# Pairs of batches in rows of their own: wider product matmuls, 64-row products with the states, four groups in place of five, and another tabulated order

## The chip, the cores and the metric

The kernel runs on one NeuronCore of a Trainium2 chip. The metric is the device time of one execution in microseconds (us). The engines are TensorE (PE for matmuls, PEld for the weight load ahead of each), VectorE (DVE), ScalarE (ACT), GpSimd (POOL) and SyncE (SP), whose queue issues nearly all DMAs.

## The reference, cut to what matters

Eight batches of eight heads; x is (8, 8, 512, 64), state (8, 8, 32, 64), all float32. An attention between tokens and states in both directions gives 544 rows of 512 per batch, and a soft mixture of experts runs over all 4352 rows.

```python
scores = x @ state.T / 8;  a  = softmax(scores);   xread = a @ state
scores2 = state @ x.T / 8; a2 = softmax(scores2);  sread = a2 @ x
x = concat([xread, sread], axis=2)             # then (B, S + Ns, H * D)
logits = x @ phi                               # 32 slots
d = softmax(logits over all rows)              # dispatch
slot_input = d.T @ x
slot_out[e] = relu(slot_input[e] @ w1[e]) @ w2[e]     # 8 experts, 4 slots each
out = softmax(logits over slots) @ slot_out    # combine
```

## The kernel before, in words

The kernel never forms xread. It folds the states into phi (`G`: state times phi, for every head), so that the logits of the tokens are G times the attention weights. The dispatch product d.T @ xread is taken in two steps as well: first the 32x32 blocks t = d.T @ a of each head (`T`), then t @ state (`Px`). The softmax over all rows is a running one: for each group of batches a new maximum, a factor that rescales what was summed so far, and an addition to the 128x128 tile `y`, which becomes the slot inputs.

Each batch b goes through steps, which are small functions. `X.b.g` transposes two heads of x on PE (g from 0 to 3) and `xe` copies them out on ACT; `S.b` makes the scores; then, for each half h of the heads, the token softmax (`q` transpose on DVE, `m1` maximum on DVE, `sub` on POOL, `x1` exponential on ACT, `l1`, `r1` on DVE, `mul` on POOL, `aT` transpose on DVE), the state softmax (`m2` on DVE, `e2` on ACT, `l2` on DVE) with its transposes (`E` on PE, `ee` on ACT) and its product with x (`R` on PE, then `sr`, `srT`, `srTe`), and the logits `Lx.b.h` on PE from `aT` and G. `A.b.h` transposes `aT` back on PE and `ae` copies it out on ACT, into one of two `an` buffers.

A group k of batches (the table `GROUPS`) then goes through `keep`, `mx` (maximum), `mk`, `bm`, `nme` (maximum over the rows of the array), `dx` (exponential on ACT), `dT`, `dTe` (transpose and copy), `T`, `tt` (transpose on DVE), `Px`, and `Y` (the addition to y). The state rows of four batches each go through a like chain (`Ls` to `Ys`). `Wd`, `We`, `Yf`, `SI`, `SIe` close the softmax and place the slot inputs in `si_m`; then come the expert matmuls `w1_half` (tile h_ps), `w2_part` (so_ps) and `out` (o).

What sets the order is `ORDER`, a written list of some 480 steps: each engine executes its instructions in the order in which this list issues them. Loads of expert weights are issued by SP as the buffers of x come free: `R.b.1` issues two of them, `load_half` puts three half sets into buffers of the attention, and the rest follow in the expert stage.

Of the kernel before, what the change touches and what calls it, by code (L numbers as in the profile page):

```python
# [34 lines left out]
X.3.0 r1.1.0 mul.1.0 xe.3.0 x1.1.1 A.0.1 R.1.0 Lx.0.0 m2.2.0 R.1.1 l2.1 Lx.0.1 X.4.1 e2.2.1 m1.2.0 sub.2.0
aT.1.0 E.2.1 q.2.1 ae.0.1 l1.1.1 A.1.0 e2.2.0 l2.2 ee.2.1 r1.1.1 xe.4.1 S.3 X.4.0 sr.1 srTe.0 m1.2.1 X.4.3
ae.1.0 m2.3.0 mul.1.1 aT.1.1 E.2.0 x1.2.0 xe.4.0 srT.1 l1.2.0 xe.4.3 U.0 m2.3.1 X.4.2 q.3.0 ee.2.0 sub.2.1
e2.3.0 Lx.1.0 R.2.0 srTe.1 q.3.1 Lx.1.1 Ue.0 R.2.1 sr.2 xe.4.2 m1.3.0 sub.3.0 A.1.1 E.3.0 e2.3.1 keep.0 X.5.3
r1.2.0 mx.0 m1.3.1 S.4 sub.3.1 x1.2.1 l1.2.1 m2.4.0 mk.0 bm.0 nme.0 srT.2 xe.5.3 X.5.2 m2.4.1 ee.3.0 x1.3.0
# [5 lines left out]
sub.5.1 E.5.0 l1.4.0 r1.4.1 msx.0 lkp.0 pv.1 V.0 sr.4 r1.4.0 dsx.0 l1.5.0 mul.4.0 x1.5.1 al.0 S.6 aT.3.1 m2.6.0
ee.5.0 Px.0 ee.5.1 Ve.0 l1.5.1 m2.6.1 r1.5.1 mul.5.1 mul.4.1 Y.0 R.5.0 r1.5.0 Lx.3.1 mx.1 l2.5 e2.6.0 keep.1
R.5.1 A.3.1 X.7.0 e2.6.1 ae.3.1 q.6.1 mk.1 srT.4 srTe.4 aT.5.1 sr.5 xe.7.0 X.7.1 xe.7.1 X.7.2 xe.7.2 bm.1 X.7.3
E.6.1 nme.1 dx.1 q.6.0 xe.7.3 al.1 als.0 srT.5 D.0 E.6.0 dT.1 srTe.5 dTe.1 m1.6.0 sub.6.0 pv.2 mul.5.0 aT.4.0
ee.6.0 x1.6.0 l2.6 m1.6.1 sub.6.1 S.7 aT.4.1 Lu.0 m2.7.1 C.0 Ce.0 A.5.1 Lx.4.0 m2.7.0 aT.5.0 T.1 ee.6.1 Lx.4.1
tt.1 R.6.0 e2.7.1 x1.6.1 l1.6.0 Lx.5.0 Ps.0 l1.6.1 ae.5.1 Lus.0 Lx.5.1 mx.2 R.6.1 e2.7.0 A.4.0 keep.2 E.7.0  # L50
r1.6.1 mul.6.1 E.7.1 mk.2 Ys.0 bm.2 ae.4.0 ee.7.0 sr.6 r1.6.0 mul.6.0 q.7.0 srT.6 A.4.1 nme.2 aT.6.1 m1.7.0
ee.7.1 U.1 aT.6.0 dx.2 pv.3 q.7.1 A.5.0 dT.2 l2.7 srTe.6 dTe.2 Lu.1 R.7.0 Lx.6.0 ae.5.0 R.7.1 sub.7.0 x1.7.0
Lx.6.1 keep.3 Px.1 ae.4.1 m1.7.1 sr.7 srT.7 mx.3 mk.3 Y.1 Ue.1 load_half A.6.0 bm.3 A.6.1 srTe.7 Ls.1 sub.7.1
x1.7.1 l1.7.0 r1.7.0 mul.7.0 nme.3 al.3 l1.7.1 al.2 Lse.1 r1.7.1 aT.7.0 T.2 dx.3 dT.3 dTe.3 Lr.1 ae.6.1 lkp.1
# [14 lines left out]
def attention_soft_moe(ctx: ExitStack, tc: tile.TileContext, x, stT, phi, w1, w2, out_x, out_s):  # L69
# [84 lines left out]
    with ExitStack() as actx:  # L154
# [27 lines left out]
        def G(b):  # L182
            R[0]["gp"] = p = ps_t.tile([P, B, 2 * NS], F32, tag="tr", name="g_ps")
            for b in range(B):
                for g in range(4):
                    pe.matmul(
                        p[32 * g : 32 * g + 32, b, :],
                        stT_sb[:, b, 32 * g : 32 * g + 32],
                        phi_bd[:, g].rearrange("p h n -> p (h n)"),
                        start=True,  # L190
                        stop=True,
                    )
# [25 lines left out]
        def Sc(b):  # L218
# [3 lines left out]
            for g in range(4):  # L222
                for h in range(2):
                    pe.matmul(  # L224
                        r[f"sp{h}"][32 * g : 32 * g + 32, :],
                        stT_sb[64 * h : 64 * h + 64, b, 32 * g : 32 * g + 32],
# [231 lines left out]
        def T_(k):  # L458
            r = X2[k]
            r["tp"] = mtile([P, len(r["b"]), 2, NS], f"t_ps{k}")  # L460
            for i, b in enumerate(r["b"]):
                for j in range(NJ):
                    for g in range(4):
                        pe.matmul(  # L464
                            r["tp"][32 * g : 32 * g + 32, i, :, :],
                            r["dT"][:, i, 32 * j : 32 * j + 32],
                            R[b]["an"][:, j, g],
# [4 lines left out]
        def tt(k):  # L472
            r = X2[k]
            r["tt"] = sm.tile([P, len(r["b"]), 2, NS], F32, tag="tt", name=f"tt_{k}", bufs=1)
            dve.transpose(
                r["tt"].rearrange("p i h n -> p (i h n)"), r["tp"].rearrange("p i h n -> p (i h n)")
# [12 lines left out]
        def Px(k):  # L489
            r = X2[k]  # L490
            r["pxp"] = p = mtile([P, 2, D], f"px_ps{k}")
            n = len(r["b"])
            for h in range(2):
                for g in range(4):
                    rows = slice(32 * g, 32 * g + 32)
                    for i, b in enumerate(r["b"]):
                        pe.matmul(
                            p[rows, h, :],
                            r["tt"][rows, i, h, :],
                            Q[b // 4]["st"][rows, b % 4, D * h : D * h + D],  # L500
                            start=(i == 0),
                            stop=(i == n - 1),
# [325 lines left out]
```

## Time and profile before

| | us |
|---|---|
| median of 3 timed runs (150.08 to 151.0) | 150.22 |
| the profiled execution, whole | 151.79 |
| its span in the trace | 150.0 |
| attention and dispatch: start to the first h_ps matmul | 93.1 |
| first expert matmuls (h_ps) | 14.25 |
| from there to the end | 42.7 |

| engine | busy us | share of the span | instructions |
|---|---|---|---|
| PE | 124.9 | 83% | 2083 |
| PEld | 93.9 | 63% | 2083 |
| DVE | 88.4 | 59% | 223 |
| ACT | 88.0 | 59% | 210 |
| POOL | 41.9 | 28% | 61 |

The shares are means over two unlike halves: up to 93 us all engines work side by side, and behind it DVE and ACT wait for PE and PE works through the expert weights. The mean granted clock of TensorE is 0.95. DMA moves 51.76 MB in all, and stands nearly still from 86 to 95 us.

### The profile page before, as it was taken

What the parts mean: (1) busy time and instruction counts of PE and PEld (TensorE: products, weight loads), DVE (VectorE), ACT (ScalarE), POOL (GpSimd) and SP (SyncE); (2) the same over time, 40 slices, a digit from 0 to 9 for tenths busy, and PEclk for the clock granted to TensorE, in tenths of its full rate; (3) what the DMA queues carried; (4) which work ended last, traced back from release to release, by engine and by line L of the source; (5) the groups of instructions that cost most, each with busy time, mean ns of one, the idle gap of its engine ahead of it and who ended that gap; (6) DMA issues with size and microseconds to landing.
All of it is one profiled execution on the core that took longest, in us unless ns stands there. A gap on an engine that the chain in (4) does not pass through costs nothing.

```text
span 150.0 us, 5037 instructions
## 1 busy us (share of the span) xinstructions
PE 124.9 (83%) x2083; PEld 93.9 (63%) x2083; DVE 88.4 (59%) x223; ACT 88.0 (59%) x210; POOL 41.9 (28%) x61
## 2 busy tenths in 40 slices
PE   0598939999999998599996787999999999988700
PEld 0567735977677856549874564999786656656500
DVE  2019990999799999759986216198220143356700
ACT  3149963996999985969984821206430445366700
POOL 3004543262555563381847120630000000000000
PEclk9999995999999999969999969999999999999985
DMA  4899999999999999999999800289999938668995
GB/s 120 289 387 402 420 414 421 413 420 415 414 415 415 418 416 417 416 418 413 404 402 304 317 20 2 82 298 390 421 420 415 421 152 352 281 256 350 418 420 238
DMA packets 15286, 51.76 MB, mean 345 GB/s; under 512 B 1696, under 2 KB 1952, under 8 KB 15264
## 3 DMA queue, kind: packets, MB, share of 16 engines
q1 hardware_dynamic: 15120, 51.39, 86.6%
q8 instruction: 16, 0.26, 0.7%
q10 hardware_dynamic: 144, 0.07, 0.2%
q14 instruction: 6, 0.05, 0.1%
HBM read 42.53 MB, written 8.91 MB: 343 GB/s over the span
## 4 chain that ended last, share of the span: by engine, by line
PE 68%; DVE 12%; issue 6%; ACT 6%; DMA 3%; SPq 0%; DVEq 0%; ACTq 0%
PE so_ps L701 10%; PE h_ps L646 9%; PE xt_ps L210 8%; PE sc L224 6%; PE o L731 6%; PE eT_ps L292 4%; PE an_ps L292 4%; PE sr_ps L317 4%; PE t_ps L464 3%; DMA x<-x_in 3%; ACT out L733 2%; PE lt L349 2%; PE cT_ps L686 2%; DVE q L237 2%; DVE l1s L253 2%
## 5 line engine op out<-in xcount | busy, mean ns | idle before, releaser
L210 PE MATMUL xt_ps<-ident,x 128*128 128x128 f32 x128 | 20.5, 303 | 9.5 <-DMA x<-x_in 5.6
L210 PEld LDWEIGHTS xt_ps<-ident,x 128*128 128x128 f32 x128 | 15.7, 154 | 14.5 <-issue 9.1
L215 ACT ACTIVATE xt<-xt_ps 128x512 f32<-128x512 f32 x32 | 18.5, 612 | 7.0 <-PE xt_ps L210 6.5
L262 POOL TENSOR_TENSOR q<-q,r 128x512 f32<-128x512 f32 x16 | 16.7, 1048 | 18.0 <-DVE r L258 10.5
L246 POOL TENSOR_TENSOR q<-q,m 128x512 f32<-128x512 f32 x16 | 16.7, 1049 | 16.5 <-DVE m L242 9.3
L273 DVE TENSOR_REDUCE nm<-sc 128x1 f32<-128x512 f32 x16 | 10.5, 667 | 12.2 <-PE sc L224 12.2
L735 DVE COPY out<-o 128x512 f32<-128x512 f32 x16 | 10.8, 689 | 9.6 <-PE o L731 9.6
L733 ACT COPY out<-o 128x512 f32<-128x512 f32 x18 | 10.3, 586 | 8.4 <-PE o L731 8.3
L701 PE MATMUL so_ps<-w,h_m 128*32 128x256 f32 x256 | 15.3, 382 | 0.0
L646 PE MATMUL h_ps<-w,si_m 128*32 128x512 f32 x128 | 14.2, 592 | 0.4 <-DVE si_m L624 0.4
L731 PE MATMUL o<-so,cT 128*128 128x256 f32 x68 | 12.7, 313 | 1.8 <-ACT out L733 0.9
L646 PEld LDWEIGHTS h_ps<-w,si_m 128*32 128x32 f32 x128 | 12.9, 110 | 1.0 <-DVE si_m L624 0.5
L731 PEld LDWEIGHTS o<-so,cT 128*128 128x128 f32 x68 | 9.4, 188 | 6.5 <-ACT out L733 2.4
L278 ACT ACTIVATE e<-sc,nm 128x512 f32<-128x512 f32 x16 | 11.3, 704 | 1.5 <-DVE q L237 1.2
L267 DVE STREAM_TRANSPOSE aT<-q 128x512 f32<-128x512 f32 x16 | 11.1, 692 | 1.6 <-PE eT_ps L292 0.8
L237 DVE STREAM_TRANSPOSE q<-sc 128x512 f32<-128x512 f32 x16 | 11.0, 690 | 1.0 <-ACT e L278 0.9
L309 ACT COPY an<-an_ps 128x512 f32<-128x512 f32 x16 | 9.3, 590 | 3.1 <-PE an_ps L292 3.1
L224 PE MATMUL sc<-xt,stT_sb 64*32 64x512 f32 x128 | 11.0, 690 | 0.0
L317 PE MATMUL sr_ps<-x,eT 128*32 128x64 f32 x512 | 10.5, 221 | 0.5 <-ACT eT L300 0.5
L701 PEld LDWEIGHTS so_ps<-w,h_m 128*32 128x32 f32 x256 | 7.7, 109 | 5.1 <-issue 0.3
L292 PE MATMUL eT_ps<-ident,e 128*128 128x128 f32 x64 | 10.1, 291 | 0.9 <-ACT e L278 0.5
L242 DVE TENSOR_REDUCE m<-q 128x16 f32<-128x512 f32 x16 | 10.6, 668 | 0.1
(127 smaller groups left out, 206.7 us busy)
## 6 DMA issues: line engine op xcount, KB each, us to landing
w<-w_in SPq DMA_DIRECT2D x61, 512.0 KB, 9.9
out_x<-out SPq DMA_DIRECT2D x16, 512.0 KB, 3.5
x<-x_in SPq DMA_DIRECT2D x14, 512.0 KB, 9.1
w<-w_in SPq DMA_DIRECT2D x6, 256.0 KB, 7.5
...
```

Source lines behind the costliest of these rows:

```text
L210: pe.transpose(p[:, P * j : P * j + P], xb[2 * b + g // 2][:, g % 2, j, :], ident)
L215: act.mul(r[f"xt{g}"], r[f"xp{g}"], 0.125)
L224: pe.matmul(r[f"sp{h}"][32 * g : 32 * g + 32, :], stT_sb[64 * h : 64 * h + 64, b, 32 * g : 32 * g + 32], r[f"xt{g}"][64 * h : 64 * h + 64, :],
L237: dve.transpose(r[f"q{h}"], r[f"sp{h}"])
L246: pool.tensor_tensor(v, v, R[b][f"m1{h}"].broadcast_to([P, 16, NS]), op=ALU.subtract)
L262: pool.tensor_tensor(v, v, R[b][f"r1{h}"].broadcast_to([P, 16, NS]), op=ALU.mult)
L292: pe.transpose(p[:, j, :], r[f"{src}{h}"][:, P * j : P * j + P], ident)
L317: pe.matmul(r["srp"][32 * g : 32 * g + 32, h, :], r[f"eT{h}"][:, j, 32 * g : 32 * g + 32], xb[2 * b + g // 2][:, g % 2, j, D * h : D * h + D],
L646: pe.matmul(h_ps[hf][32 * kt : 32 * kt + 32, :], si_m[kt // 2][:, 256 * (kt % 2) + 32 * e : 256 * (kt % 2) + 32 * e + 32], w1t[4 * e + kt] ...
L701: pe.matmul(so[hf][c4 : c4 + 32, :], h_m[ft // 4][:, 256 * (ft % 4) + 32 * e : 256 * (ft % 4) + 32 * e + 32], w2t[hf, e, ft], start=(e == ...
L731: pe.matmul(o[:, i, :], cT[b // 2][:, 4 * (b % 2) + j + i, :], so4[hf], start=True, stop=True)
L733: act.copy(ot[:, j : j + 2, :], o)
```

## The change

The change concerns the dispatch products `T` and `Px` and what they need. The last two batches, groups of their own before, become one pair, so there are four groups of two. In `T` the two batches of a pair no longer lie side by side in the free dimension, with the four head pairs g in the four row blocks of the output; now a row block of 32 holds (half of g, batch), and the two g of a half lie side by side in the free dimension. A matmul therefore streams 128 columns instead of 64, and there are half as many. In `Px` the two batches lie under each other in 64 contraction rows, so the sum over the pair, which took two accumulating matmuls, takes one. For this the states are stored in another order (`stT_in`, read through `st_t`), and the first of their two loads holds two batches (128 KB) in place of one (64 KB). `Y`, `mx`, `dx` and the others are as before, four times instead of five.

```diff
-GROUPS = ((0, 1), (2, 3), (4, 5), (6,), (7,))
+GROUPS = ((0, 1), (2, 3), (4, 5), (6, 7))
...
-    stT_sb = big.tile([P, B, P], F32, tag="big", name="stT_sb")
+    stT_sb = big.tile([P, 4, 2, 2, 2, NS], F32, tag="big", name="stT_sb")
...
+    def st_t(b, g):
+        return stT_sb[:, b // 2, g % 2, g // 2, b % 2, :]
...
-            r["tp"] = mtile([P, len(r["b"]), 2, NS], f"t_ps{k}")
-            for i, b in enumerate(r["b"]):
-                for j in range(NJ):
-                    for g in range(4):
+            r["tp"] = mtile([P, 2, 2, NS], f"t_ps{k}")
+            for j in range(NJ):
+                for gh in range(2):
+                    for i, b in enumerate(r["b"]):
+                        row = 64 * gh + 32 * i
                         pe.matmul(
-                            r["tp"][32 * g : 32 * g + 32, i, :, :],
+                            r["tp"][row : row + 32, :, :, :],
                             r["dT"][:, i, 32 * j : 32 * j + 32],
-                            R[b]["an"][:, j, g],
+                            R[b]["an"][:, j, 2 * gh : 2 * gh + 2],
...
-            for h in range(2):
-                for g in range(4):
-                    rows = slice(32 * g, 32 * g + 32)
-                    for i, b in enumerate(r["b"]):
+            for g2 in range(2):
+                for h in range(2):
+                    for gh in range(2):
+                        g = 2 * gh + g2
+                        rows = slice(64 * gh, 64 * gh + 64)
                         pe.matmul(
-                            p[rows, h, :],
-                            r["tt"][rows, i, h, :],
-                            Q[b // 4]["st"][rows, b % 4, D * h : D * h + D],
-                            start=(i == 0),
-                            stop=(i == n - 1),
+                            p[32 * g : 32 * g + 32, h, :],
+                            r["tt"][rows, g2, h, :],
+                            Q[k // 2]["st"][rows, 2 * (k % 2) + g2, D * h : D * h + D],
+                            start=True,
+                            stop=True,
                         )
...
-X.0.1 xe.0.1 X.0.0 X.0.2 X.0.3 xe.0.0 xe.0.2 xe.0.3 S.0 m2.0.0 X.1.1 xe.1.1 q.0.0 m1.0.0 sub.0.0 X.1.0 xe.1.0
+X.0.0 xe.0.0 X.0.1 xe.0.1 X.0.2 xe.0.2 X.0.3 xe.0.3 S.0 m2.0.1 X.1.1 xe.1.1 m2.0.0 q.0.0 m1.0.0 sub.0.0 e2.0.1
```

The new list moves steps all over the attention. Two places matter below. The first is on PE, early: the step `G` (tile g_ps, 32 short matmuls) stood between the two `R` steps of batch 0 (sr_ps), with the transposes of batch 3 behind them. Of the program before:

```order
L317 MATMUL sr_ps_348<-x_0_66,eT_0_322 32x64 x2
L317 MATMUL sr_ps_348<-x_1_69,eT_0_322 32x64 x2
...
L186 MATMUL g_ps<-phi_bd,stT_sb 32x64 x32
L317 MATMUL sr_ps_348<-x_0_66,eT_1_398 32x64 x2
L317 MATMUL sr_ps_348<-x_1_69,eT_1_398 32x64 x2
...
L210 MATMUL xt_ps_2_428<-ident,x_1_84 128x128 x4
L210 MATMUL xt_ps_3_435<-ident,x_1_84 128x128 x4
L292 MATMUL an_ps_0_444<-ident,aT_0_433 128x128 x4
```

And of the changed program, where the two `R` steps of batch 0 come behind the rows shown:

```order
L294 MATMUL eT_ps_1_285<-ident,e_0_1_252 128x128 x4
L188 MATMUL g_ps<-phi_bd,stT_sb 32x64 x32
L226 MATMUL sc_0_331<-xt_0_283,stT_sb 32x512
L226 MATMUL sc_1_332<-xt_0_283,stT_sb 32x512
...
L212 MATMUL xt_ps_1_345<-ident,x_0_78 128x128 x4
L294 MATMUL eT_ps_0_353<-ident,e_0_0_272 128x128 x4
L212 MATMUL xt_ps_0_362<-ident,x_0_78 128x128 x4
L212 MATMUL xt_ps_3_373<-ident,x_1_80 128x128 x4
L212 MATMUL xt_ps_2_383<-ident,x_1_80 128x128 x4
L319 MATMUL sr_ps_392<-x_0_66,eT_0_360 32x64 x2
```

`G` now stands ahead of the scores of batch 1 (sc), and the short matmuls of `R` come after four more transposes.

The second place is the end of the dispatch on PE, from the logits of the last half (lt, made from aT_1 of batch 7) to the experts. Of the program before:

```order
L349 MATMUL lt_1727<-aT_1_1735,G_sb 32x128 x4
L292 MATMUL an_ps_1_1766<-ident,aT_1_1735 128x128 x4
L292 MATMUL an_ps_0_1772<-ident,aT_0_1675 128x128 x4
L384 MATMUL bm_ps_1782<-mk_1777,rep 128x5
L464 MATMUL t_ps_1785<-an_1723,dT_1715 32x64 x16
L566 MATMUL v_ps_1808<-ident,srT_1252 128x128 x4
L451 MATMUL dT_ps_1819<-ident,dx_1814 128x128
L497 MATMUL px_ps_1821<-st_1627,tt_1806 32x64 x8
L464 MATMUL t_ps_1838<-an_1802,dT_1836 32x64 x16
L577 MATMUL ps_ps_1861<-srN_1855,D_1817 32x128 x4
L594 MATMUL l_ps<-l_row,rep 128x1
L497 MATMUL px_ps_1872<-st_1627,tt_1859 32x64 x8
```

Of the changed program, where the sixteen matmuls of a `T` step are cut to two rows:

```order
L351 MATMUL lt_1586<-aT_1_1626,G_sb 32x128 x4
L468 MATMUL t_ps_1644<-an_1550,dT_1578 32x128
L468 MATMUL t_ps_1644<-an_1478,dT_1578 32x128
...
L294 MATMUL an_ps_0_1661<-ident,aT_0_1572 128x128 x4
L386 MATMUL bm_ps_1674<-mk_1634,rep 128x5
L294 MATMUL an_ps_1_1682<-ident,aT_1_1591 128x128 x4
L294 MATMUL an_ps_1_1687<-ident,aT_1_1626 128x128 x4
L454 MATMUL dT_ps_1698<-ident,dx_1693 128x128 x2
L571 MATMUL v_ps_1703<-ident,srT_1346 128x128 x4
L502 MATMUL px_ps_1709<-st_1640,tt_1680 32x64 x8
L468 MATMUL t_ps_1720<-an_1678,dT_1701 32x128
...
```

The product `T` of batches 4 and 5 now stands behind the last logits, with three of the four `A` transposes of batches 6 and 7, and one `T` of the pair stands where two of single batches stood.

More of the change, by code (lines that the diff above doesn't have):

```diff
@@ L35 @@
[L35 to L39, printed above, removed]
@@ L45 @@
[L45 to L49, printed above, removed]
@@ L50 @@
[L50 to L54, printed above, removed]
@@ L55 @@
-mul.7.1 Lx.7.0 tt.2 ae.6.0 aT.7.1 Px.2 Lx.7.1 Lu.2 msx.1 dsx.1 A.7.1 keep.4 A.7.0 pv.4 mx.4 mk.4 bm.4 Y.2 T.3
-ae.7.1 nme.4 ae.7.0 tt.3 V.1 als.1 dx.4 D.1 dT.4 Px.3 Lu.3 al.4 Lus.1 Y.3 dTe.4 T.4 Ve.1 Lu.4 tt.4 Ps.1 Ys.1 Wd
-We Px.4 C.1 windows Y.4 Yf SI SIe Ce.1
+X.0.0 xe.0.0 X.0.1 xe.0.1 X.0.2 xe.0.2 X.0.3 xe.0.3 S.0 m2.0.1 X.1.1 xe.1.1 m2.0.0 q.0.0 m1.0.0 sub.0.0 e2.0.1
+X.1.2 X.1.3 xe.1.3 xe.1.2 q.0.1 m1.0.1 e2.0.0 sub.0.1 l2.0 X.1.0 xe.1.0 E.0.1 x1.0.0 l1.0.0 G.0 r1.0.0 ee.0.1
+mul.0.0 S.1 m2.1.0 Ge.0 x1.0.1 X.2.1 l1.0.1 q.1.1 E.0.0 xe.2.1 ee.0.0 X.2.0 xe.2.0 r1.0.1 mul.0.1 X.2.3 m1.1.1
@@ new lines @@
+l1.2.0 srT.1 xe.4.3 sr.2 r1.2.1 mul.2.1 q.3.0 X.4.2 xe.4.2 E.3.0 m1.3.1 sub.3.1 e2.3.1 A.1.1 ae.1.1 keep.0 bm.0
+nme.0 A.1.0 ae.1.0 dx.0 S.4 r1.2.0 ee.3.0 X.5.2 m1.3.0 l2.3 m2.4.1 xe.5.2 E.3.1 ee.3.1 srTe.1 srT.2 mul.2.0
+q.4.0 X.5.0 aT.2.0 X.5.3 xe.5.0 X.5.1 sub.3.0 x1.3.0 m1.4.0 dT.0 aT.2.1 srTe.2 al.0 A.2.0 xe.5.1 R.3.0 l1.3.0
+m2.4.0 Lx.2.0 q.4.1 R.3.1 sub.4.0 Lx.2.1 dTe.0 T.0 r1.3.0 xe.5.3 X.6.1 mul.3.0 x1.3.1 l1.3.1 m1.4.1 e2.4.0
+r1.3.1 sub.4.1 e2.4.1 A.2.1 aT.3.0 ae.2.0 x1.4.0 ae.2.1 xe.6.1 S.5 E.4.0 tt.0 ee.4.0 X.6.0 sr.3 srT.3 E.4.1
@@ new lines @@
+m2.5.1 l2.4 x1.4.1 X.6.3 mul.3.1 q.5.0 Lx.3.0 R.4.0 aT.3.1 Lx.3.1 l1.4.0 xe.6.0 srTe.3 Ls.0 m1.5.0 sub.5.0
+ee.4.1 A.3.0 X.6.2 e2.5.1 R.4.1 xe.6.3 m2.5.0 Lse.0 l1.4.1 e2.5.0 r1.4.0 xe.6.2 Lr.0 q.5.1 E.5.1 ae.3.0 x1.5.0
+msx.0 ee.5.1 lkp.0 dsx.0 r1.4.1 mul.4.1 m1.5.1 X.7.0 l2.5 l1.5.0 keep.1 als.0 sub.5.1 sr.4 mul.4.0 E.5.0 ee.5.0
+mx.1 pv.1 S.6 m2.6.1 xe.7.0 Px.0 X.7.3 Y.0 A.3.1 e2.6.1 R.5.0 mk.1 xe.7.3 q.6.1 ae.3.1 aT.4.1 V.0 Ve.0 m2.6.0
+e2.6.0 R.5.1 X.7.1 aT.4.0 E.6.1 q.6.0 m1.6.1 sub.6.1 xe.7.1 X.7.2 xe.7.2 bm.1 E.6.0 r1.5.0 Lu.0 x1.5.1 S.7 nme.1
@@ new lines @@
+m1.6.0 ee.6.0 l2.6 R.6.0 dx.1 ee.6.1 l1.5.1 C.0 q.7.0 r1.5.1 x1.6.1 Ce.0 m2.7.1 R.6.1 m2.7.0 srT.4 srTe.4 Lx.4.0
+sr.5 mul.5.0 srT.5 e2.7.0 aT.5.0 srTe.5 e2.7.1 m1.7.0 mul.5.1 Lx.4.1 E.7.0 ee.7.0 sr.6 Lx.5.0 E.7.1 sub.6.0
+sub.7.0 aT.5.1 dT.1 x1.7.0 q.7.1 dTe.1 srT.6 A.4.0 srTe.6 A.5.0 Lus.0 x1.6.0 l1.6.1 m1.7.1 Lx.5.1 keep.2 l1.7.0
+l1.6.0 mx.2 l2.7 R.7.0 ee.7.1 sub.7.1 r1.7.0 mul.7.0 x1.7.1 T.1 pv.2 mk.2 ae.5.0 tt.1 R.7.1 sr.7 A.5.1 ae.5.1
+r1.6.1 r1.6.0 mul.6.0 load_half bm.2 nme.2 srT.7 srTe.7 mul.6.1 A.4.1 Ls.1 dx.2 l1.7.1 ae.4.1 aT.7.0 r1.7.1 dT.2
@@ L58 @@
+U.1 A.7.0 aT.6.0 Lse.1 D.0 dTe.2 Lr.1 Lx.6.0 aT.6.1 lkp.1 msx.1 mul.7.1 Lx.6.1 Ps.0 ae.4.0 dsx.1 Lx.7.0 Px.1
+al.1 al.2 aT.7.1 Lx.7.1 Lu.1 pv.3 windows Ue.1 Ys.0 Y.1 T.2 A.6.0 Lu.2 mx.3 mk.3 als.1 Lus.1 bm.3 ae.7.0 ae.6.0
+tt.2 A.6.1 A.7.1 nme.3 dx.3 ae.6.1 ae.7.1 dT.3 dTe.3 V.1 al.3 Px.2 Y.2 keep.3 T.3 Ve.1 D.1 Ps.1 tt.3 Ys.1 Lu.3
+Wd We Px.3 Y.3 C.1 Yf SI Ce.1 SIe
 """
@@ L812 @@
         "x_in": con(x.reshape(B, 4, 2, NJ, P, D).transpose(0, 4, 1, 3, 2, 5)).reshape(B, P, NJ * 8 * D),
-        "stT_in": con(state.reshape(B, 4, 2, NS, D).transpose(2, 4, 0, 1, 3)).reshape(P, B, P),
+        "stT_in": con(state.reshape(4, 2, 2, 2, 2, NS, D).transpose(4, 6, 0, 3, 2, 1, 5)).reshape(P, 4, 2, 2, 2, NS),
         "phi_in": con(moe_phi.reshape(4, 2, D, NS).transpose(1, 2, 0, 3)).reshape(P, 4, NS),
```

28 lines of the change are left out of this document (12 added, 16 removed).

## The prediction

> **What bounds the kernel now.** I read the page first, then the chain that ended last, then the table by stretches of time, and last the DMA queues in short windows. PE counts most of the chain, but 6% of it is "issue", time in which the engine waited for nothing that the profile shows.
>
> ```profile
> PE 124.9 (83%) x2083; PEld 93.9 (63%) x2083; DVE 88.4 (59%) x223; ACT 88.0 (59%) x210; POOL 41.9 (28%) x61
> q8 instruction: 16, 0.26, 0.7%
> PE 68%; DVE 12%; issue 6%; ACT 6%; DMA 3%; SPq 0%; DVEq 0%; ACTq 0%
> ```
>
> Pieces of the chain (start, length, what) show where the issue time sits:
>
> ```profile
> 19.49 0.37 PE xt_ps L210 x2
> 19.86 2.38 issue
> ...
> 78.66 0.57 PE t_ps L464 x34
> 79.23 1.35 issue
> 80.59 0.65 PE t_ps L464 x30
> ...
> 84.67 0.56 PE t_ps L464 x27
> 85.23 1.56 issue
> 86.80 0.31 PE t_ps L464 x5
> 87.11 1.04 PE v_ps L566 x4
> 88.15 0.21 PE dT_ps L451
> 88.37 0.58 PE px_ps L497 x16
> 88.94 1.01 PE t_ps L464 x32
> ```
>
> Three gaps, together 5.29 us, each break a step in its middle: two of four transposes, 34 of 64 T matmuls, 27 of 32. Nothing that an engine computes can be missing there. The queue q8 tells what is. It moved 0.26 MB in 16 packets while PE and PEld executed 2 x 2083 = 4166 instructions, that is 260 per packet. These are q8's rows in the 0.2 us windows that begin at 19.8, 78.0 and 84.4 us, in this order:
>
> ```profile
> q8 instruction: 1, 0.02, 27.5%
> q8 instruction: 1, 0.02, 29.2%
> q8 instruction: 1, 0.02, 29.3%
> ```
>
> The gaps end at 22.23, 80.58 and 86.80: each about 2.4 us behind such a packet. So I read a gap as PE at the end of a block of some 256 instructions, whose successor is still on its way. The stretch table (PE, PEld, DVE, ACT, POOL busy, with counts; granted clock; DMA share; GB/s) gives the size of a block and what the gaps cost:
>
> ```profile
> 17.50:22.00 4.50, 2.36 (x130) 2.13 (x131) 4.47 (x11) 3.71 (x9) 1.51 (x3) 1.00 1.03 417
> 20.00:25.00 5.00, 2.77 (x18) 2.12 (x25) 2.34 (x7) 1.73 (x4) 2.73 (x3) 0.72 1.02 413
> 22.20:25.80 3.60, 3.57 (x26) 2.12 (x25) 0.17 (x1) 1.08 (x2) 1.64 (x2) 0.53 1.03 421
> 70.00:75.00 5.00, 4.89 (x113) 4.43 (x107) 4.93 (x15) 4.39 (x14) 3.15 (x5) 1.00 1.03 407
> 80.40:86.70 6.30, 4.63 (x126) 3.47 (x127) 2.07 (x7) 4.06 (x15) 2.09 (x10) 1.00 0.84 299
> 86.70:93.00 6.30, 5.21 (x89) 3.72 (x88) 2.34 (x11) 1.34 (x3) 0.74 (x2) 0.73 0.02 7
> ```
>
> Between the ends of the last two gaps stand 126 + 127 = 253 instructions, and they held 4.63 us of PE work: the next block took 6.2 us from one crossing to the next (80.58 to 86.80). The first gap: 261 instructions with 2.36 us of work from 17.5 on, the next block there 4.7 us later. A block therefore comes 4.7 to 6.2 us after the crossing ahead of it while the DMA share is near 1, and a block with less PE work than that makes PE wait. Without such a wait the attention is a balance: from 70 to 75 us PE, DVE and ACT are busy 4.89, 4.93 and 4.39 of 5.
>
> [...]
>
> **The change, part by part.** The whole is counted from the span of the profiled execution, 150.0; that execution took 151.79, so 1.8 us lie around the span. The timed median is 150.22, near the span by chance, and I set the sum against the median.
>
> *Fewer instructions.* A matmul that does not transpose is two passes, each with a weight load, so four instructions. T falls from 128 matmuls to 64 and Px from 64 to 32: 96 x 4 = 384 instructions, one and a half blocks. The streaming time hardly moves:
>
> ```profile
> 68.21 0.89 PE t_ps L464 x64
> 69.10 0.22 PE lt L349 x8
> 82.28 0.61 PE px_ps L497 x30
> ```
>
> T of a pair was 0.89. Now it is four rounds of four 128-column matmuls side by side, as one Lx is (0.22): 4 x 0.22 = 0.88. A single T was about half, so batches 6 and 7 together cost the same. Px of a pair was 0.61; the new eight matmuls use two row groups where sixteen used four. The trace has no 64-row, 64-column product; two at a time, four rounds of half an Lx, 0.44, is one bound and 0.61 the other. I take 0.5.
>
> *Gap 1 (2.38).* The block that ran out held R, G and R. In the new order the same stretch of 254 instructions runs from the middle of G to E.1.0 and holds S.1, four X, E.0.0 and both R:
>
> ```profile
> 18.07 0.97 PE g_ps L186 x64
> 38.80 1.10 PE sc L224 x16
> 42.06 0.59 PE xt_ps L210 x4
> 43.43 0.58 PE sr_ps L317 x32
> 44.01 0.59 PE eT_ps L292 x4
> ```
>
> 0.5 + 1.10 + 4 x 0.59 + 0.59 + 2 x 0.58 = 5.7 us against 4.7 to 6.2 needed, and E.1.0 waits for an exponential on ACT, which comes near 20 us in either order because ACT is full there. DVE and ACT stood idle 2.66 and 3.27 of the five us from 20 to 25. Ends: 0 and -3.2. I take -1.9, the gap less half a us of wait that may remain.
>
> *Gap 2 (1.35).* It is paid where DVE waits: the transpose tt.2 stands ahead of the last aT in DVE's queue.
>
> ```profile
> 81.29 0.32 DVE L475 STREAM_TRANSPOSE tt<-t_ps 128x128 f32<-128x128 f32 x1 [0.95 <-PE t_ps L464]
> 81.53 0.67 DVE L267 STREAM_TRANSPOSE aT<-q 128x512 f32<-128x512 f32 x1
> ```
>
> DVE lost 0.95 there. In the new order T.2 stands behind that aT, so I take -0.95; ends 0 and -1.35.
>
> *One group fewer.* DVE and ACT lose a mx, a nme, a Y, half a tt, and ACT a keep, a mk, an al and part of dx:
>
> ```profile
> L365 DVE TENSOR_REDUCE mx<-lt 128x1 f32<-128x256 f32 (+1 forms) x5 | 1.8, 356 | 2.0 <-ACT lt_all L359 2.0
> L421 DVE SCALAR_TENSOR_TENSOR y<-y,al_all,px_ps 128x128 f32<-128x128 f32 x4 | 1.4, 345 | 2.1 <-PE px_ps L497 2.0
> L441 ACT ACTIVATE dx<-lt,nm_all 128x256 f32<-128x256 f32 (+1 forms) x5 | 2.3, 451 | 0.0
> ```
>
> About 0.9 us on DVE, of which I count -0.6 on the path, since DVE is full but not alone; ends 0 and -0.9.
>
> *The tail, from the last aT (ends 82.20) to the experts.* Before, 10.9 us:
>
> ```profile
> 93.10 14.25 PE h_ps L646 x128
> ```
>
> Gap 3 is 1.56 of it. Behind it the clock is 0.73 on the mean: V took 1.04, and T of one batch 1.01 where half of 0.89 is the full speed, Px of one batch 0.58 against 0.30: another 1.3 us. Without both it is 8.0. The new tail, step by step: Lx.7.1 to 0.35 us after aT; T.2 to 1.25; then ACT has two ae (0.59 each, they wait for T.2's `an` buffers) to 2.55, dx with its read to 3.2, two more ae to 4.25, dTe 0.37 to 4.6; T.3 to 5.65; tt to 6.1; Px to 6.7; Y, Yf, SI and SIe 1.5 us, as from 91.63 to 93.10, to 8.2. The pair's wider chain thus pays back what a group less saves. I take -2.5; -1.4 if the slow clock stays, -3.3 at best.
>
> [...]
>
> *The start.* X.0.0 comes first, whose data were issued 0.43 us ahead of those that PE waited for:
>
> ```profile
> 1.16 4.30 DMA x<-x_in
> 5.59 3.38 PE xt_ps L210 x16
> ```
>
> The doubled state load (128 KB) shares the queues, another 64 KB, 0.25 us at the 250 GB/s or so that the core moves then. I take -0.3; ends +0.25 and -0.6.
>
> *New fetch waits.* By the same addition the lightest blocks of the new order hold 4.9 us (R.6.1 to T.1), 5.3 (to Px.1), 5.7 (to Px.3), 5.7 (above) and 5.9. At 4.7 us for a block none waits, at 6.2 they wait 3.5 in all. But the attention has other waits: 12 blocks took 88 us before, 7.3 each. I take +0.8.
>
> *The rest* (experts, output) moves as one: its loads are set off by its own matmuls, and DMA stood still from 86 us on (2% of its engines from 86.7 to 93.0), so 5 us less of pause hides no load. If loads still ran then, the shift would be lost up to their length; I price that in the range.
>
> Sum: -1.9 - 0.95 - 0.6 - 2.5 - 0.3 + 0.8 = -5.45; 150.22 - 5.45 = **144.8**.
>
> **The rivals.**
>
> *All is gained.* The gaps vanish with DVE's 2.66 us of idleness, the tail comes at its best, no new wait: -2.7 - 1.35 - 0.9 - 3.3 - 0.3 = -8.5, 141.7. For it speaks the balance of the engines; against it that three full engines seldom keep all that one is given.
>
> *The gaps are not fetches of blocks, or come back elsewhere.* Then half as many matmuls of twice the width change nothing, and the group saved and the start give -0.9 to -1.5: 149. For it speaks that only three of some twelve crossings show a gap; against it the packets 2.4 us ahead of each gap's end. [...]
>
> *Slower: the blocks come later than PE wants them, five times.* The new order spreads 2766 instructions of the attention more evenly, so that no block is far too light, but five lie at 4.9 to 5.9 us. If a block takes 7 us, they wait 2.1 + 1.7 + 1.3 + 1.3 + 1.1 = 7.5, more than the 5.3 removed and the 0.9 of group and start: 150.2 + 7.5 - 6.2 = 151.5. It decides from 6.7 us per block on; the trace shows 4.7 and 6.2.
>
> **How the numbers follow.** 0.56 for the forecast (143 to 147.5), 0.14 for the full gain, 0.18 for 149, 0.12 for the slower case. The range 141.6 to 149.5 leaves out the last and little of the first two. Within 1% (148.7 to 151.7) is about what a measurement of this kernel cannot tell from no change; two thirds of the case at 149 lie in it, so 0.12; faster 0.76, slower 0.12.
>
> **What will show it.** Right: no issue time of over 1 us on PE ahead of the experts, DVE busy over 4 of 5 us from 20 to 25, h_ps first at 87 to 89, T of a pair at 0.85 to 0.95 in 32 records, 15 packets on q8, the stretch from h_ps to the end unchanged at 57 us. Wrong: gaps in the middle of R, T or Px that end 2.4 us behind a q8 packet, or a DVE that waits for POOL or ACT in the middle of the attention, which I haven't followed step by step.

## The result, and the profile after

| | before | after |
|---|---|---|
| median of the timed runs, us | 150.22 (three, 150.08 to 151.0) | 142.09 (four, 140.69 to 142.44) |
| ratio, 95% interval | | 0.9428 (0.934 to 0.9516) |
| profiled execution, whole / span | 151.79 / 150.0 | 140.69 / 138.9 |
| last aT ends | 82.20 | 72.13 |
| first h_ps matmul | 93.10 | 80.32 |
| from there to the end of the span | 56.9 | 58.6 |

The change took 8.1 us off the median, and 5.7% by the ratio. The two profiled executions differ by 11.1, because before's was 1.6 above its median and after's, the shortest of its four, 1.4 below. So pieces read from the traces add up to more than the timed gain. Executions more than 1.5% above the fastest of the same kernel are left out of all medians and ratios; of the changed kernel with G late, below, that leaves a single run, which is not the profiled one, and no ratio.

These rows of the page of the changed kernel answer to the first ones shown of before:

```profile
PE 118.8 (86%) x1889; PEld 89.1 (64%) x1889; DVE 86.4 (62%) x219; ACT 86.7 (62%) x203; POOL 41.5 (30%) x59
q8 instruction: 15, 0.25, 0.7%
PE 44%; DVE 29%; ACT 10%; issue 5%; DMA 4%; SPq 1%; POOL 1%; DVEq 0%; ACTq 0%; POOLq 0%
```

PE has 194 matmuls and 194 weight loads less, 388 where 384 were expected of T and Px (the bm of one group makes the other four), and q8 has one packet less. DVE's share of the chain rose from 12% to 29%: in the attention the chain now goes from one DVE instruction to the next. "issue" is still 5% of the chain, but in many small pieces, none longer than 0.61 us. No gap of over 1 us on PE without a releaser is left.

Stretches of time, before (two rows) and after (three); columns as in the prediction's stretch table:

```profile
10.00:70.00 60.00, 54.52 (x1102) 39.99 (x1100) 50.59 (x123) 50.10 (x123) 28.05 (x31) 0.94 1.03 415
60.00:70.00 10.00, 8.49 (x173) 6.26 (x177) 7.49 (x18) 8.80 (x25) 4.84 (x8) 0.83 1.02 416
```

```profile
10.00:70.00 60.00, 57.54 (x1156) 43.47 (x1155) 57.19 (x145) 55.51 (x138) 32.77 (x36) 1.00 1.03 416
20.00:25.00 5.00, 5.00 (x117) 3.62 (x115) 4.97 (x11) 4.26 (x10) 2.19 (x3) 1.00 1.02 415
60.00:70.00 10.00, 9.06 (x177) 7.14 (x178) 9.83 (x29) 8.37 (x24) 7.24 (x9) 1.00 1.03 417
```

Of these 60 us DVE stood idle for 9.4 before and 2.8 after, and the clock is at 1.00 throughout. From 20 to 25 us, where the first gap was, DVE is busy 4.97 of 5. But the stretch from 60 to 70 recovers almost as much (7.49 to 9.83), and no block gap of before lies there. The prediction had not looked at it.

The tail, in the chain of the changed kernel:

```profile
70.42 0.72 DVE aT L269
71.19 0.43 PE lt L351 x8
...
72.42 0.36 PE lt L351 x8
72.78 0.94 PE t_ps L468 x32
73.75 1.11 ACT an L311 x2
74.86 0.48 ACT dx L443 x2
75.38 0.44 PE dT_ps L454 x2
...
76.63 1.07 PE t_ps L468 x32
...
80.07 0.20 DVE si_m L629
80.32 14.25 PE h_ps L651 x128
```

The last aT of all runs from 71.42 for 0.71, so the tail is 80.32 - 72.13 = 8.2 us, with the steps in the predicted order: T.2, two ae, dx, T.3. The two T of a pair in it take 0.94 and 1.07, each in 32 records.

The end. DMA issues (KB each, median us to landing), before and then after:

```profile
out_x<-out SPq DMA_DIRECT2D x16, 512.0 KB, 3.5
out_s<-out SPq DMA_DIRECT2D x2, 256.0 KB, 3.6
```

```profile
out_x<-out SPq DMA_DIRECT2D x16, 512.0 KB, 4.8
out_s<-out SPq DMA_DIRECT2D x2, 256.0 KB, 5.4
```

The last copies of `out` come 48.84 us behind the first h_ps in both kernels, yet the span ends 1.7 us later behind them. The stretches of the changed kernel's end (last two columns: DMA share, GB/s):

```profile
134.00:135.00 1.00, 0.00 (x0) 0.00 (x0) 0.00 (x0) 0.00 (x0) 0.00 (x0) 0.50 1.00 412
135.00:136.00 1.00, 0.00 (x0) 0.00 (x0) 0.00 (x0) 0.00 (x0) 0.00 (x0) 0.50 0.71 273
136.00:137.00 1.00, 0.00 (x0) 0.00 (x0) 0.00 (x0) 0.00 (x0) 0.00 (x0) 0.50 0.06 25
137.00:138.00 1.00, 0.00 (x0) 0.00 (x0) 0.00 (x0) 0.00 (x0) 0.00 (x0) 0.50 0.03 12
```

A share of 0.06 is one of the sixteen DMA engines. It works alone for another 1.8 us while the other fifteen are done.

### The profile page after: what moved, and what is told of

It reads as the page before. It is cut to its first block, busy times and chain, and to the rows that moved or that the text cites. A ratio compares the mean times of both kernels' runs of the same rounds, so it can differ in the third digit from the quotient of the medians.

```text
span 138.9 us, 4645 instructions
## 1 busy us (share of the span) xinstructions
PE 118.8 (86%) x1889; PEld 89.1 (64%) x1889; DVE 86.4 (62%) x219; ACT 86.7 (62%) x203; POOL 41.5 (30%) x59
## 3 DMA queue, kind: packets, MB, share of 16 engines
HBM read 42.53 MB, written 8.91 MB: 370 GB/s over the span
## 4 chain that ended last, share of the span: by engine, by line
PE 44%; DVE 29%; ACT 10%; issue 5%; DMA 4%; SPq 1%; POOL 1%; DVEq 0%; ACTq 0%; POOLq 0%
PE so_ps L706 11%; PE h_ps L651 10%; PE o L736 6%; DVE aT L269 5%; DVE q L239 5%; DVE l1s L255 4%; DMA x<-x_in 4%; DVE m L244 4%; PE xt_ps L212 3%; DVE nm L275 3%; ACT e L280 3%; ACT out L738 3%; DVE r L260 2%; PE cT_ps L691 2%; PE sc L226 2%
## 5 line engine op out<-in xcount | busy, mean ns | idle before, releaser
L212 PE MATMUL xt_ps<-ident,x 128*128 128x128 f32 x128 | 19.9, 296 | 5.1 <-DMA x<-x_in 4.9
L217 ACT ACTIVATE xt<-xt_ps 128x512 f32<-128x512 f32 x32 | 19.0, 613 | 6.1 <-PE xt_ps L212 6.1
L212 PEld LDWEIGHTS xt_ps<-ident,x 128*128 128x128 f32 x128 | 15.1, 150 | 10.5 <-issue 6.2
L280 ACT ACTIVATE e<-sc,nm 128x512 f32<-128x512 f32 x16 | 11.1, 697 | 2.0 <-DVE nm L275 1.2
L239 DVE STREAM_TRANSPOSE q<-sc 128x512 f32<-128x512 f32 x16 | 11.1, 692 | 0.9 <-ACT e L280 0.9
L269 DVE STREAM_TRANSPOSE aT<-q 128x512 f32<-128x512 f32 x16 | 10.9, 685 | 0.0
L251 ACT ACTIVATE q<-q 128x512 f32<-128x512 f32 x16 | 10.3, 642 | 0.8 <-POOL q L248 0.8
L255 DVE TENSOR_REDUCE l1s<-q 128x16 f32<-128x512 f32 x16 | 10.5, 662 | 0.3 <-ACT q L251 0.3
L319 PE MATMUL sr_ps<-x,eT 128*32 128x64 f32 x512 | 10.1, 220 | 0.0
```

Source lines behind the costliest of these rows:

```text
L212: pe.transpose(p[:, P * j : P * j + P], xb[2 * b + g // 2][:, g % 2, j, :], ident)
L217: act.mul(r[f"xt{g}"], r[f"xp{g}"], 0.125)
L239: dve.transpose(r[f"q{h}"], r[f"sp{h}"])
L255: dve.tensor_reduce(out=l1s[:, i, :, 0:1], in_=R[b][f"qv{h}"], axis=AX.X, op=ALU.add)
L269: dve.transpose(r[f"aT{h}"], r[f"q{h}"])
L280: act.activation(r[f"e2{h}"], r[f"sp{h}"], AF.Exp, bias=r[f"nm2{h}"], accum_out=l2s[:, b % 2, h, 0:1])
```

## The experiments

All twelve, by the trace's landmarks, in the order told. "Body end" is the end of the last aT. The kernels with loads later or gated were run once each.

| kernel | median us | ratio (95%) | body end | first h_ps | h_ps to end |
|---|---|---|---|---|---|
| changed, narrow products | 147.16 | 0.9797 (0.9701 to 0.9894) | 75.53 | 88.72 | 56.9 |
| old list, four groups, narrow | 148.98 | 0.9868 (0.9804 to 0.9931) | 81.45 | 89.78 | 57.0 |
| old list, four groups, wide | 147.7 | 0.9852 (0.9739 to 0.9965) | 78.58 | 86.62 | 58.4 |
| the same, G early | 145.93 | 0.9721 (0.9643 to 0.9799) | 77.56 | 85.60 | 58.6 |
| the same, keep.1 late too | 145.85 | 0.9666 (0.9581 to 0.975) | 76.32 | 85.40 | 59.8 |
| before, G early | 148.35 | 0.9885 (0.9844 to 0.9926) | 81.51 | 90.76 | 56.9 |
| changed, G late | 143.4 | | 77.55 | 85.74 | 58.6 |
| before, loads later in the list | 151.99 | | 82.55 | 93.29 | 56.9 |
| before, loads gated | 195.4 | | 81.55 | | |
| changed, loads gated | 187.77 | | 72.83 | | |
| changed, 28 PE instructions more | 138.8 | 0.9237 (0.9186 to 0.9288) | 71.79 | 79.98 | 56.9 |
| changed, 64 PE instructions more | 139.9 | 0.9286 (0.9242 to 0.9329) | 72.58 | 80.77 | 57.3 |

**The changed kernel with narrow matmuls.** The products are cut back to the old width, with order, groups and layout kept. That is 384 PE instructions more.

```diff
+            for g2 in range(2):
...
-                            r["tp"][row : row + 32, :, :, :],
+                                r["tp"][row : row + 32, g2, :, :],
...
-                            R[b]["an"][:, j, 2 * gh : 2 * gh + 2],
+                                R[b]["an"][:, j, 2 * gh + g2],
...
+                            for c in range(0, D, 32):
```

> The changed kernel with its T matmuls cut back to 64 columns and its Px matmuls cut to 32: the same products, the same order and the same streaming time, but 96 more matmuls (384 more instructions). Blocks (PE waits for the next block of some 256 instructions): by adding the steps, one block from T.1 to R.7.1 then holds only 1.9 us of PE work and the one that ends in T.3 3.9; gaps of 2 to 4 us in R.7.1 and of about 1 us in T.3 return, h_ps starts 2 to 4.5 us later than at 80.3, the time is 144 to 146.5. Order (the gain comes from how the new list fills the engines, the gaps were by the way): no gap above 1 us, within 1 us of the changed kernel.

It took 5.1 us more than the changed kernel (147.16 against 142.09), beyond what I had expected. Two rows of its chain, and PE around the first of them:

```profile
66.64 2.56 issue
...
76.57 2.77 issue
```

```profile
66.01 0.63 PE L319 MATMUL sr_ps<-x,eT 128*32 128x64 f32 x32
69.19 0.88 PE L294 MATMUL an_ps<-ident,aT 128*128 128x128 f32 x4 [2.56 <-issue]
```

Gaps come back, one behind R, one in the middle of T.2 (expected in T.3), 5.3 us together. Behind each of them PE runs at half clock:

```profile
69.50:72.90 3.40, 3.40 (x24) 2.69 (x22) 2.06 (x6) 2.26 (x7) 0.75 (x2) 0.50 1.03 423
79.70:83.10 3.40, 3.40 (x53) 3.23 (x42) 0.48 (x2) 1.79 (x5) 0.00 (x0) 0.50 1.05 399
```

So h_ps comes 8.4 us later (88.72 against 80.32), where 2 to 4.5 had been expected. The gaps are 5.3 of it; the other 3.1 fit the slow clock, since two times 3.4 us at half speed cost up to 3.4. The end is 1.7 us shorter, and the medians differ by 5.1. The list in itself doesn't keep the gaps away; the number of instructions does.

**The old list with four groups, narrow and wide.** The table of before, without the steps of group 3 (batch 6 alone); those of group 4 serve the pair. In the first kernel the products are narrow, in the second wide.

```diff
-pv.3
...
-keep.3
...
-T.2 dx.3 dT.3 dTe.3
+T.2
...
-keep.4 A.7.0 pv.4 mx.4 mk.4 bm.4 Y.2 T.3
+keep.3 A.7.0 pv.3 mx.3 mk.3 bm.3 Y.2
```

> Four groups on the list of before, as the kernel with the changed products on that list, but with T cut to 64 columns and Px to 32: 384 instructions more. Blocks: the gap of 2.4 us near 20 us, and gaps of 2 to 3 us in T.2 (the block holds 3.1 us of PE work) and about 1.5 us in T.3; the time 1 to 2.5 us above that with the wide products (149 to 151). The group alone (against the kernel before, 150.7): 0 to 1.3 us less. If wide products save by themselves, beyond the blocks, the two differ by more than the gaps.

> The changed kernel's products and four groups with the list of steps of before, from which group 3's steps are taken out, with group 4's, now the pair's, left where they stood. Blocks: the gap of 2.4 us in X.3.2 stays (the stretch holds 2.3 us of PE work as before), the lightest blocks behind it hold 4.4 and 4.7 us, so gaps 2 and 3 shrink under 1 us each; h_ps at about 93.1 - 1.35 - 1.56 - 1.3 - 0.6 = 88 to 89, time 145 to 147. Order: with the list of before at most the group saved is gained, h_ps at 91.5 to 93, time 148.5 to 150.5.

The longest issue pieces of the narrow one, then of the wide one:

```profile
20.13 2.38 issue
...
77.52 2.30 issue
```

```profile
19.85 2.33 issue
...
75.45 1.08 issue
```

One group less gives 1.3% by itself, about 2 us, more than the 0 to 1.3 expected. In the traces h_ps comes 3.3 us earlier, 0.75 of it in the body. The rest is the tail: it falls from 10.9 to 8.3, since the gap (1.56) and the slow clock (0.73 on the mean from 86.7 to 93.0 us in before) ahead of the last T are gone. The gap of 1.5 us that was expected in T.3 didn't come. The wide products then shorten gap 2 from 2.30 to 1.08 and bring h_ps another 3.2 us forward, to 86.62, earlier than the 88 to 89 of the theory of blocks. But at the end the wide one loses 1.4 us (58.4 against 57.0): its time, 147.7, lies between the range of that theory (145 to 147) and the one of the order (148.5 to 150.5), and the ratios of the two kernels, 0.9868 and 0.9852, can't be told apart. So on the old list the wide matmuls are worth little that can be timed.

**G early in the program of before, and late in the changed one.** Only two steps of the table move.

The first:

```diff
-e2.0.1 E.0.0 m1.0.1 sub.0.1 x1.0.0 l2.0
+e2.0.1 E.0.0 G.0 m1.0.1 sub.0.1 x1.0.0 Ge.0 l2.0
...
-R.0.0 G.0 ee.0.1 R.0.1 e2.1.0 m1.1.0 sub.1.0 xe.2.3 Ge.0
+R.0.0 ee.0.1 R.0.1 e2.1.0 m1.1.0 sub.1.0 xe.2.3
```

> The kernel before with two steps moved: G directly behind E.0.0 and Ge behind x1.0.0. Nothing else. Blocks: the stretch that held 2.3 us of PE work up to X.3.2 holds 5.6, the gap at 19.86 falls under 0.6 us, gaps 2 and 3 stay; h_ps 1.5 to 2.6 us earlier than at 93.1, time 147.5 to 149. Order: the gap is the mark of a wait elsewhere and moves to another place, the time stays within 0.7 of the kernel before.

The second:

```diff
-l1.0.0 G.0 r1.0.0 ee.0.1 mul.0.0 S.1 m2.1.0 Ge.0 x1.0.1
+l1.0.0 r1.0.0 ee.0.1 mul.0.0 S.1 m2.1.0 x1.0.1
...
-R.0.0 R.0.1
+R.0.0 G.0 Ge.0 R.0.1
```

> The changed kernel with G and Ge moved back between the two R steps of batch 0, nothing else. Blocks: that stretch holds 2.3 us of PE work again, and a gap of 1.8 to 2.8 us returns on PE near 20 us, in E.1.0 or just ahead of it; h_ps 1.5 to 2.6 us later than at 80.3, time 143.5 to 145. Order: no gap, or one that costs nothing, the time within 0.7 of the changed kernel.

In before the first gap goes, and h_ps comes 2.34 us earlier. But of this the body end has only 0.7, since a new gap opens behind:

```profile
66.36 1.15 issue
...
77.55 1.92 issue
...
90.76 14.25 PE h_ps L653 x128
```

Two other steps were hit, by block borders that moved as I read it, where the gaps in T.2 and T.3 had been expected to stay. The time fell by 1.15%. With G late in the changed kernel PE waits again near 20 us:

```profile
PE xt_ps L218 <- issue: 3.0, 1, 3.0
```

Its h_ps comes 5.4 us later in the profiled execution (1.5 to 2.6 expected), but that execution took 146.15 us against 143.4 in the table, which is 1.3 above the changed kernel. So the gap is shown, its price in time is not.

**The old list, four groups, wide, with G early.** To the wide kernel on the old list it adds the move of G that was shown for the program of before.

```diff
-e2.0.1 E.0.0 m1.0.1 sub.0.1 x1.0.0 l2.0
+e2.0.1 E.0.0 G.0 m1.0.1 sub.0.1 x1.0.0 Ge.0 l2.0
```

> The changed kernel's products and four groups with the list of steps of before (group 3's steps taken out), and G and Ge moved early as well. So all that was named of the change is there but the rest of the new list. Blocks: no gap near 20 us, one of about 1 us left in T.2; the time about 2 us under that of the same kernel without the move (146.5 to 147.5). If the blocks were all of the gain it would reach the changed kernel (142 to 143); what it stays above that is the rest of the list: fewer us in which DVE is idle. I expect 3 to 5 us of that.

The one long issue piece left is the 1.08 in T.2. The time is 1.8 us under that of the same kernel without the move. At 145.93 it stands 3.8 us above the changed kernel, inside what was expected for the rest of the new list. So with two of the three gaps gone and the third short, a good part of the gain is still missing. Its trace shows one reason, which stands in before's trace too. Before first, ACT and PE, and then this kernel's:

```profile
59.86 0.37 ACT L359 COPY lt_all<-lt 128x256 f32<-128x256 f32 x1 [1.56 <-DVE mx L365]
61.44 0.66 PE L210 MATMUL xt_ps<-ident,x 128*128 128x128 f32 x4 [1.45 <-ACT an L309]
```

```profile
57.22 0.37 ACT L367 COPY lt_all<-lt 128x256 f32<-128x256 f32 x1 [1.56 <-DVE mx L373]
58.80 0.66 PE L218 MATMUL xt_ps<-ident,x 128*128 128x128 f32 x4 [1.45 <-ACT an L317]
```

keep.1, a copy of logits, stands behind mx.1 in the old list. ACT waits 1.56 us until DVE gets to mx.1. Behind the copy stand the exponential and the `ae` that PE's next transposes need.

**keep.1 later.** The last run moves that one step.

```diff
-Lx.3.1 mx.1 l2.5 e2.6.0 keep.1 R.5.1
+Lx.3.1 mx.1 l2.5 e2.6.0 R.5.1
...
-nme.1 dx.1 q.6.0 xe.7.3
+nme.1 dx.1 q.6.0 xe.7.3 keep.1
```

> As the old list with four groups, wide products and G early (145.93, h_ps first at 85.60), with one step moved: keep.1, ACT's copy of the logits of batches 2 and 3, stands behind xe.7.3 in place of ahead of the exponential e2.6.1. There ACT stood idle 1.56 us until DVE had done mx.1, and PE behind it 1.45 us. Theory (a wait of this list, not a block, which the new list doesn't have): both waits go, h_ps first 1.0 to 1.8 us earlier, at 83.8 to 84.6, whole time 144 to 145. Rival (ACT and DVE are short of work there anyway, and another step waits in its place): h_ps at 85.2 to 85.8, time 145.5 to 146.3.

Both waits are gone, and the last aT ends 1.24 us earlier (76.32 against 77.56), as the theory has it. But h_ps comes only 0.2 earlier, and the median is the rival's. The trace of this kernel says why, in rows of its tail and of the chain:

```profile
80.50:81.00 0.50, 0.25 (x10) 0.26 (x14) 0.00 (x0) 0.50 (x2) 0.50 (x3) 1.00 1.05 414
81.50:82.00 0.50, 0.50 (x16) 0.50 (x12) 0.00 (x0) 0.00 (x0) 0.00 (x0) 0.50 1.00 389
```

```profile
85.40 15.56 PE h_ps L657 x128
```

The granted clock fell to 0.50 at 81.5 us, in the middle of T.3, and came back at 88.3. The steps from T.3 on took 1.0 us longer, the h_ps stage 1.2 (15.56 against 14.38 in the kernel it is compared with). So the wait is a cause, worth 1.2 us in the body; that it pays in the time was not shown: in the profiled run a slow clock took the gain back, the other runs have no trace, and the intervals of the two ratios (0.9666 and 0.9721) overlap.

**Are the gaps the DMA load's doing?** The first attempt put the issues of the expert weights later in the program of before.

```diff
-        load_w(NBIG - 2 * B - 1)
...
+        load_w(NBIG - 2 * B - 1)
+        load_half()
```

> The kernel before with 26 of its loads of expert weights and the three half loads held back until the last step of the attention has been issued: same PE instructions, but DMA has only x and 17 weight tiles to move before the experts, and the experts then wait for their weights, so the whole time is worse (above 165) and only the attention is read. If a block is late because its fetch stands behind weight transfers: the gap at 19.86 stays (x is still being loaded), the gaps in T.2 and T.3 shrink from 1.35 and 1.56 to under 0.5, the slot inputs are ready 2 to 4 us earlier than at 93.1. If the fetch is slow by itself, both gaps stay.

This tells nothing on its question: SP ran ahead through the list and issued the loads all the same, with the DMA queues as full as before up to 80 us (410 GB/s from 30 to 80 us, 411 in before). What it did show is that the gaps repeat, in the same three steps, in another execution. The second attempt makes the loads wait for an instruction of POOL behind the last step of the attention, in both kernels.

```diff
             t = big.tile([P, F], F32, tag="big", name=f"w{i}_{e}_{k}")
+            if not w1t:
+                pool.memset(t[:, 0:1], 0.0)
...
+        load_w(NBIG)
+        load_half()
```

> The kernel before with all loads of expert weights behind one write by POOL that comes after its last step of the attention, so that DMA is idle from the end of x (about 25 us) to the end of the dispatch. The experts then wait for their weights; the whole time is 160 to 175 and only the attention is read, up to the slot inputs (si_m). If a block of instructions is late because it queues behind weight transfers: the gap of 2.4 us near 20 us stays, since x is still being loaded; the gaps in T.2 and T.3 vanish; the slot inputs come 2.5 to 4.5 us earlier than at 93.1. If the fetch is slow by itself: both gaps stay, 93 us.

> The changed kernel with the same hold on the weights. It has no gap of a block that could go, so its slot inputs come at 79.5 to 80.5 as in the changed kernel; time 150 to 165. The difference to the kernel before with the same hold, less the first gap, is then what the new list and one group less are worth without any late block: 6 to 8 us. If a good part of the changed kernel's gain were hidden waits for blocks, this run would be faster too, by 1 us or more.

The whole times are of no use here (the loads now come late, and 195.4 is more than the 160 to 175 expected). The attention is what counts. In before with gated loads the DMA engines stand nearly still in the rest of the attention (a share of 0.57 from 20 to 30 us, of 0.01 to 0.02 and 2 to 6 GB/s from 30 to 80), and one issue row is left on PE:

```profile
PE xt_ps L218 <- issue: 2.4, 1, 2.4
```

That is gap 1, at 20 us, where x itself is still being loaded. The gaps in T.2 and T.3 are gone, and the slot inputs (si_m) are written at 88.7 instead of 92.9. Before, then before and the changed kernel with gated loads:

```profile
92.86 0.48 DVE L624 COPY si_m<-si_ps 128x32 f32<-128x32 f32 x4 [0.56 <-PE si_ps L606]
```

```profile
88.70 0.48 DVE L630 COPY si_m<-si_ps 128x32 f32<-128x32 f32 x4 [0.55 <-PE si_ps L612]
81.10 0.48 DVE L635 COPY si_m<-si_ps 128x32 f32<-128x32 f32 x4 [0.92 <-PE si_ps L617]
```

So gaps 2 and 3 cost 4.2 us with the slow clock behind them, and they came with a loaded DMA (a share of 1.02 from 30 to 80 us in before) and not with one at rest. The body end is 81.55, against 82.20, so 0.65 of it (gap 2) lie in the body and 3.5 in the tail. In the changed kernel with gated loads the slot inputs come at 81.1 instead of 80.1 (79.5 to 80.5 expected); 0.7 of this stands already at the scores of batch 1 (15.09 against 14.39). So no hidden wait for blocks was seen in it to be won. Between the two gated kernels stand 7.6 us, of which gap 1 is 2.4. Behind gap 1 the granted clock is 0.50 for 3.4 us, which costs up to 1.7 us more. So some 3.5 to 5 us of the gain have nothing to do with late blocks.

**More PE instructions at the start.** Transposes of the identity into an unused buffer while PE waits for x: 14 of them in one kernel, 10 and 11 one-column matmuls in another. They add nothing to any result.

```diff
+        warm = ps_t.tile([P, 4, P], F32, tag="tr", name="warm")
+        for i in range(14):
+            pe.transpose(warm[:, i % 4, :], ident, ident)
...
         order = ORDER.split()
```

> The changed kernel with 14 transposes of the identity on PE while x is on its way (from 1.4 to about 4.4 us; 28 instructions more, their output is read by nobody). Clock: the transposes of batch 0, 0.85 us a step, and S.0, 1.74, run at full speed (0.59 and 1.1), S.0 ends 0.5 to 1 us earlier, since the last of the four is held by its data until 7.7; time 141 to 141.7. Order and blocks: lightest block 5.2 us in place of 4.9, no new gap. If the first steps are bound by data alone: no change.

> As the one with 14 transposes, but with 10 transposes and 11 one-column matmuls: 64 instructions more than the changed kernel. The changed kernel's outputs end with one or two DMA engines 1.5 us behind the others, and its last block of instructions is fetched at 125 us, in the midst of the last outputs. If that fetch holds an engine's outputs back, here it comes at about 119 to 120, where the queues are partly idle, and the stretch from the first h_ps to the end is 57 us in place of 58.6: time 139.5 to 140.5. If not, the stretch stays and the time is that of the run with 14 transposes.

Both beat the changed kernel, the first with 138.8 and a ratio of 0.9237 (0.9186 to 0.9288), the best version of this study and 2.2 us under the least that was expected of it (141). Its start:

```profile
1.35 3.10 PE L641 MATMUL warm<-ident 128*128 128x128 f32 x14 [1.35 <-POOL ident masks.py:199]
4.29 0.60 PE L212 MATMUL xt_ps<-ident,x 128*128 128x128 f32 x4
```

An X step takes 0.60 to 0.65 instead of 0.85, but PE waits for x between them (0.23 to 0.41 us), S.0 takes 1.80 us as in the changed kernel (1.1 expected), and h_ps comes only 0.34 us earlier. The other 1.7 us of its profiled execution, which had not been expected, are at the end, 56.9 against 58.6: the lone DMA engine is gone. In the second kernel the four X steps take 3.74 us together (3.38 in before), and h_ps comes 0.45 us later than in the changed kernel, so all of its gain is at the end. With these instructions the last q8 packet moves. It comes 40.1 us behind the first h_ps in the first of the two kernels, 45.1 in the changed kernel, 34.7 in before. For eleven kernels with a normal end:

| last q8 packet behind h_ps, us | h_ps to end, us |
|---|---|
| 34.7 to 35.0 (before, its variants with G early and with loads later, both narrow kernels) | 56.9 to 57.0 |
| 38.5 (64 more), 40.1 (28 more) | 57.3, 56.9 |
| 43.1, 44.4, 45.1, 46.1 (old list wide; with G early; changed; changed with G late) | 58.4, 58.6, 58.6, 58.6 |

The kernel with keep.1 late has its packet at 45.9 and 59.8 to the end, 1.2 of it the slow clock. The output DMAs are issued from 29 to 52 us behind h_ps, the last eleven of eighteen from 41.9 on; in the changed kernel the DMA engines are full from some 44 on (a share of 1.05, 412 GB/s, from 124 to 126 us). A packet in their midst goes with an end some 1.6 us later, and the two kernels that moved the packet out moved the end back, the second by 1.3 us where 1.6 was expected. That the packet holds one engine's output back is my reading. The correlation is shown, the mechanism isn't.

## Why the prediction was right, and where not

The forecast was 144.8 (141.6 to 149.5); the time is 142.09, near the rival in which all is gained (141.7). Of the signs it named, the 15 packets, the busy DVE and the missing gaps came; h_ps came first at 80.32 and not at 87 to 89, a T of a pair took up to 1.07, and the stretch behind h_ps grew. By its own steps:

*What a gap is.* Right. Restored instructions bring gaps back (5.3 us of them, in a kernel that is 5.1 us slower), G moved takes gap 1 away or brings it back, and the gated loads remove gaps 2 and 3. The rival "not fetches of blocks" falls. Most crossings show no wait: the changed kernel has 15 packets on q8 and no gap of over 1 us. Where the block being executed held little PE work and DMA was full, pieces of 1.08 to 2.77 us stand in the chains above.

*The tail.* Right to 0.1 us: 8.2 walked, 8.19 measured, -2.7 for the term of -2.5. The kernel with four groups on the old list has 8.3, so this belongs to the group and not to the new list. The slow clock went with the gap (1.00 from 8.21 to 131.09 us, 0.73 on the mean from 86.7 to 93.0 in before), so the -1.4 that was priced for its staying did not come.

*One group fewer.* Right in kind: about -2 us by itself in the times, against -0.6 in the body (0.75 measured in the traces) and its part of the tail.

*New fetch waits, +0.8.* None came. I had priced the five lightest blocks between no wait and 3.5 us; the trace has no wait of over 1 us. The slower rival needed 6.7 us per block on five light blocks, and its point was not reached.

*The start.* -0.3 predicted; S.0 starts at 8.51 instead of 8.91, so -0.4.

*The body up to the last aT: the term that was mis-sized.* Start, gap 1, gap 2, the group and the new waits came to -2.95 (gap 2's -0.95 against 0.65 measured is the least of it); the last aT ended 10.07 us earlier. Along one path of the runs: wide products and the group on the old list -3.62, G early -1.02, the rest of the list -5.43. In the medians the last two are -1.8 and -3.8. Taken the other way round, with the new list first and G moved last, the medians give -4.3 for the list and -1.3 for G, both by the single run with G late. So the list is worth some 4 us either way.

The failing step is the one that counted the gaps alone. I priced what the trace called issue, and took the other stretches for a balance, from one window (70 to 75 us). DVE's idle time from 10 to 70 us says otherwise: 9.4 us, of which 2.66 lie where gap 1 is. In before with gated loads, where DMA stands still from some 30 us on, DVE is idle just as long there (9.6), so a loaded DMA is not what makes it idle, outside gap 1. The keep.1 wait is one such place, worth 1.24 in the body when it is removed; in before 3.4 us at half clock follow it. DVE busy from 10 to 70 goes 54.67, 55.77 and 57.19 from the kernel with it, over the one without, to the changed one. What makes up the remaining 4.2 us of the list was not taken apart, so their cause stays open. The traces only place them: against the kernel with keep.1 late the changed one is 1.6 us ahead when the scores of batch 2 start (20.46 against 22.05), 1.8 at those of batch 6 (50.00 against 51.77) and 4.2 at the last aT. So the objection that held me back from 141.7, that three full engines seldom keep what one is given, was wrong for this list.

*The rest moves as one.* Wrong by +1.7 us. I had asked whether loads ran in the pause, and they didn't hold the experts back (h_ps still 14.25). But the end went with the place of the last q8 packet, and that moved with the number of PE instructions: the change took 388 away, and the packet came 45.1 us behind h_ps in place of 34.7, among the outputs. With 384 or 28 instructions more the end is 56.9 again.

So -10.1 in the body, -2.7 in the tail and +1.7 at the end make the 11.1 between the two traces; of the sum -5.45, the body's 7 us too little and the end's 1.7 too little cancelled in part. Without the longer end the time would lie near 140.4, below the range: that the range held is luck in part.
